# The second single batch in twos of tiles, its tokens turned by VectorE in 32x32 blocks and small transfers

## The chip, the cores and the metric

The kernel runs on one core of a Trainium2 chip. The engines that matter are TensorE (PE in the profile, with its weight loads PEld), VectorE (DVE), ScalarE (ACT), GpSimd (POOL) and SyncE (SP). SP and POOL issue the DMAs here, each from its own queue. The metric is the device time of one execution in microseconds, the median of the timed runs.

## What is computed

`x` has 8 batches of 4096 tokens with 192 channels, all float32. A causal convolution with seven taps per head (8 heads of 24 channels, the taps softmaxed) is followed by a mixing over tokens and a mixing over channels, each with a residual:

```python
w = softmax(weight)                                   # 8 heads x 7 taps
xc[b, s] = sum over k of w[head, k] * x_padded[b, s + k]
h = relu(xc^T @ w_tok1) @ w_tok2                      # 4096 -> 256 -> 4096, over tokens
u = xc + h^T
out = u + relu(u @ w_ch1) @ w_ch2                     # 192 -> 1536 -> 192, over channels
```

## The kernel before

**Batches and tiles.** The eight batches go in five groups, `GROUPS = [[0], [1], [2, 3], [4, 5], [6, 7]]`: two single batches and then three pairs. A batch has NT = 8 tiles of 512 tokens, and a tile TJ = 4 blocks (j) of 128 tokens. Products run in a split form: a float32 operand is a high part plus a low part, and three products (high by high, high by low, low by high) give one.

**Stage 1 of a group** (`stage1`, L627) is the convolution of a whole batch or pair (first tap on ACT, L660, six more on VectorE, L662, in 16 pieces of the batch, stored to DRAM as `xcd`), and the first token mixing: 16 chunks of `w_tok1` are loaded (`t1_load`, L703), multiplied by the convolved tokens (`mix`, L764 for a single batch, L768 to L770 for a pair, 24 products of three kinds in the two halves of a chunk) and accumulated. For group 2 the weights come unsplit: ACT makes the high part of a chunk (L732), VectorE the low part (L736), and the convolved tokens are split by ACT (L748) and VectorE (L752). When all chunks are done, L381 and L382 make `h1`, which the second token mixing of that group reads.

**Stage 1 runs as background** of the group before it. Its steps are items with a cost, a lag and sometimes a gate (`class Item`), and the class `Background` puts them into the program between pieces of the tile work: after each piece the tile code calls `bg.fg(pe, dve)` with the piece's rough cost, and `fill` hands out the items that are due by two running sums (`bg.pe`, `bg.dve`). While `bg.tiled` is set (all of `channel1`) no item with TensorE work is handed out. Between `bg.hold()` and `bg.release()` transfers of the background wait. `bg.finish(group)` puts in whatever is left of a group's stage 1; it is called before the last tile of the group ahead.

**The tile work.** Each turn of the main loop (L1224) does one tile of one batch: `channel1` (L1039; 12 pairs of `w_ch1` blocks, products L1017, high part of the result by ACT L1056, low part by VectorE L1057), then, where the next tile is due, `mix2` of that (L891), then `channel2` (L1080; products L1091 and L1092, adds L1097 and L1098) in two halves of two blocks, and the store of the result (L1100). For a group of two batches the second product has a form with half tiles, `channel2_halves` (L1063, L1074), in those tiles in which no turn is due.

**How a next tile is made ready.** `mix2` adds the second token mixing to the convolved tokens in `u`, 128 tokens by 2x192 columns per block; `channel1` needs the channels on the partitions, so the tokens have to be turned. There are two ways, and a group uses one throughout:

- *Single batch* (groups 0 and 1). `mix2` has two products per block and half of `w_tok2` (L912, L913), two VectorE adds (L927, L928) and an ACT copy (L929): the two copies of the tile lie in `u` side by side. `transposed` (L942) turns each of the three 128-column parts with four TensorE transposes into PSUM (L950), from which ACT takes the high part (L952) and VectorE the low part (L953). It stands between the two halves of `channel2`.
- *Pair* (groups 2 to 4). `u[:, :, :, i]` holds batch i of the pair. `mix2` has three products (L915 to L917), one VectorE add (L932) and, per block, one VectorE transpose of 32x32 blocks into `own_hi` (L933). `blocks_sent` (L956) moves the blocks to their places in `other` with 16 DMAs of 48 KB, eight issued by SP and eight by POOL (L966). `parted` (L971), called in the third quarter of `channel2`, splits them (three ACT casts L979, three VectorE subtractions L981), copies the upper half of the partitions for the swapped layout (two ACT copies of 64x1536, L984) and the lower half by two POOL DMAs (L986). The first tile of the two reads `own` with its first 64 partitions and `swapped` with its last 64, the second tile the other way round.

In the pair's main loop the turn is at the second tile: the next pair's `mix2` and `blocks_sent` follow its `channel1`, and the transfers of the background are held from there until the blocks are sent.

**Loads.** `load_tile` (L868) loads the `w_tok2` part of a tile (`t2`, two DMAs, L875) and its convolved tokens (`u`, L879) on SP, one tile ahead. In group 2's stage 1 (that is, while batch 1 runs) three of the 16 chunk buffers of `w_tok1` lie in the memory of `other` (the "spare"), which batch 1 doesn't need: the last three chunks are loaded early into it (L714 to L722).

## Time and profile before

| | |
|---|---|
| median of 3 runs | 2035.07 us (2034.55 to 2036.43) |
| profiled execution: its span | 2031.3 us |
| PE busy | 2019.2 us |
| DVE busy | 1453.6 us |
| ACT busy | 761.4 us |
| POOL busy | 218.7 us |
| mean traffic | 127 GB/s |

The span of the profiled execution runs from its first to its last instruction; its own device time is not listed, and the median of the timed runs is 3.8 us longer than its span. Batch 0 takes the stretch up to about 335 us of the trace, batch 1 that from there to about 590 us, and the three pairs the rest. The places that matter are the tiles of batch 1: a tile without chunks of stage 1's product is `channel1`, `mix2` and `channel2` with the transposes in it; the next six have two chunks each; and the last four chunks stand together at the batch's end, ahead of its last tile.

### The profile page before, as it was taken

To read this page: it belongs to the slowest core of one execution; us is meant where nothing else is said; L and a number is where in the kernel's file an instruction comes from. 1 tells how busy PE (TensorE), PEld (TensorE's weight loads), DVE (VectorE), ACT (ScalarE), POOL (GpSimd) and SP (SyncE) were. 2 spreads that over 40 slices of the span, in tenths; PEclk is the share of its full clock that TensorE was granted. 3 is DMA by queue.
4 is the path that set the end of the run, shared out by engine and by line. 5 is a ranking of instruction groups with operands and counts; after the bars stand their busy time and mean duration, and the time that the engine had idled before them with its cause. 6 is when DMAs were issued, how large, how long until landed. Compare 5 with 4: busy or idle time off the path is not lost.

```text
span 2031.3 us, 42018 instructions
## 1 busy us (share of the span) xinstructions
PE 2019.2 (99%) x17435; PEld 1860.7 (92%) x17435; DVE 1453.6 (72%) x2877; ACT 761.4 (37%) x1305; POOL 218.7 (11%) x383
## 2 busy tenths in 40 slices
PE   9899999999999999999999999999999999999999
PEld 9889999999999998999999999999999999999998
DVE  8799998999659999757985689545555545555554
ACT  4575544443433434233333334233232332233322
POOL 0100000000011011100111110111111011111110
PEclk9999999999999999999999999999999999999999
DMA  9845346454434567324654434533222233233310
GB/s 308 292 158 170 119 156 201 146 168 157 142 118 134 165 199 202 104 82 128 169 162 115 108 109 134 150 87 84 73 61 56 71 84 84 76 84 84 84 48 17
DMA packets 289230, 258.39 MB, mean 127 GB/s; under 512 B 209360, under 2 KB 238544, under 8 KB 289040
## 3 DMA queue, kind: packets, MB, share of 16 engines
q1 hardware_dynamic: 265120, 168.00, 29.3%
q0 software_dynamic: 23920, 87.71, 14.0%
q8 instruction: 138, 2.26, 0.5%
q14 instruction: 52, 0.43, 0.1%
HBM read 146.60 MB, written 71.30 MB: 107 GB/s over the span
## 4 chain that ended last, share of the span: by engine, by line
PE 94%; DVE 4%; ACT 1%; DMA 0%; issue 0%; SPq 0%; POOL 0%; DVEq 0%; POOLq 0%; ACTq 0%
PE ps_x L1017 37%; PE ps_x L1091 17%; PE ps_x L1074 16%; PE ps_x L1092 8%; PE ps_x L915 2%; PE ps_x L917 2%; PE ps_x L916 2%; PE ps_a L768 2%; PE ps_a L769 2%; PE ps_a L770 2%; DVE xc L662 1%; PE ps_a L452 1%; PE ps_x L912 1%; PE ps_x L950 1%; PE ps_a L764 1%; PE ps_x L521 1%
## 5 line engine op out<-in xcount | busy, mean ns | idle before, releaser
L1056 ACT ACTIVATE hh<-ps_x 128x512 fp32r<-128x512 f32 x756 | 410.7, 596 | 744.3 <-PE ps_x L1017 744.2
L1057 DVE SCALAR_TENSOR_TENSOR hl<-ps_x,hh 128x512 fp32r<-128x512 f32 x756 | 484.9, 686 | 198.5 <-ACT hh L1056 197.0
L1091 PE MATMUL ps_x<-w,hh 128*128 128x384 f32 x1872 | 538.4, 359 | 0.1
L1092 PE MATMUL ps_x<-w,hl 128*128 128x192 f32 x1872 | 468.6, 250 | 0.0
L1017 PE MATMUL ps_x<-other,w_hi 64*128 64x512 f32 x1728 | 450.3, 389 | 0.6 <-DVE osb L1098 0.5
L662 DVE SCALAR_TENSOR_TENSOR xc<-raw,cw,xc 128x384 f32<-128x384 f32 (+1 forms) x768 | 389.4, 562 | 9.4 <-ACT xc L660 9.4
L1092 PEld LDWEIGHTS ps_x<-w,hl 128*128 128x128 f32 x1872 | 357.4, 191 | 0.0
L1091 PEld LDWEIGHTS ps_x<-w,hh 128*128 128x128 f32 x1872 | 351.5, 188 | 0.7 <-DVE hl L1057 0.7
L1017 PEld LDWEIGHTS ps_x<-other,w_hi 64*128 64x128 f32 x1728 | 314.1, 184 | 32.1 <-PE ps_x L1017 0.9
L1017 PE MATMUL ps_x<-own_hi,w_hi 64*128 64x512 f32 x1440 | 333.0, 394 | 1.2 <-DVE hl L1057 0.9
L1074 PE MATMUL ps_x<-w,hh 64*128 64x384 f32 x2304 | 329.6, 355 | 0.0
L1017 PE MATMUL ps_x<-own_hi,w_lo 64*128 64x512 f32 x1440 | 325.8, 387 | 0.0
L1017 PE MATMUL ps_x<-own_lo,w_hi 64*128 64x512 f32 x1440 | 325.6, 387 | 0.0
L1074 PE MATMUL ps_x<-w,hl 64*128 64x192 f32 x2304 | 292.2, 247 | 0.0
L1017 PEld LDWEIGHTS ps_x<-own_hi,w_hi 64*128 64x128 f32 x1440 | 210.0, 185 | 36.1 <-issue 6.3
L1017 PE MATMUL ps_x<-other,w_lo 64*128 64x512 f32 x864 | 242.1, 386 | 0.0
L1017 PEld LDWEIGHTS ps_x<-own_hi,w_lo 64*128 64x128 f32 x1440 | 215.7, 185 | 28.5
L1017 PEld LDWEIGHTS ps_x<-own_lo,w_hi 64*128 64x128 f32 x1440 | 215.8, 185 | 28.2
L1074 PEld LDWEIGHTS ps_x<-w,hl 64*128 64x128 f32 x2304 | 226.0, 188 | 1.0 <-DVE hl L1057 0.2
L1074 PEld LDWEIGHTS ps_x<-w,hh 64*128 64x128 f32 x2304 | 222.1, 184 | 0.9
L1017 PEld LDWEIGHTS ps_x<-other,w_lo 64*128 64x128 f32 x864 | 159.0, 184 | 16.1
L1097 DVE TENSOR_TENSOR osb<-ps_x,u 128x192 f32<-128x192 f32 x156 | 55.4, 355 | 143.6 <-PE ps_x L1092 143.0
(143 smaller groups left out, 2154.8 us busy)
## 6 DMA issues: line engine op xcount, KB each, us to landing
raw<-in_x_dram SPq DMA_DIRECT2D x56, 672.0 KB, 7.5
t<-t2d SPq DMA_DIRECT2D x64, 512.0 KB, 5.3
out_dram<-osb POOLq DMA_DIRECT2D x63, 384.0 KB, 4.5
u<-xcd SPq DMA_DIRECT2D x62, 384.0 KB, 6.5
xcd<-xc POOLq DMA_DIRECT2D x28, 768.0 KB, 7.6
t<-t1p SPq DMA_DIRECT2D x32, 512.0 KB, 5.4
other<-own_hi SPq DMA_DIRECT2D x192, 48.0 KB, 2.1
other<-own_hi POOLq DMA_DIRECT2D x192, 48.0 KB, 2.0
```

The costliest lines, as they stand in the source:

```text
L662: nc.vector.scalar_tensor_tensor(out=dst, in0=src, scalar=cw[:, h, k:k + 1], in1=dst, op0=ALU.mult, op1=ALU.add)
L768: nc.tensor.matmul(out=ps, lhsT=wh, rhs=xh, start=a, stop=False)
L769: nc.tensor.matmul(out=ps, lhsT=wh, rhs=xl, start=False, stop=False)
L770: nc.tensor.matmul(out=ps, lhsT=wl, rhs=xh, start=False, stop=z)
L915: nc.tensor.matmul(out=ps[:, :n], lhsT=wh, rhs=hh, start=a, stop=False)
L1017: nc.tensor.matmul(out=ps, lhsT=w1[w][rows, c, p * P:(p + 1) * P], rhs=t[h][v][rows, c], start=n == 0, stop=n == len(prods) - 1,)
L1056: nc.scalar.activation(out=h["hh", f], in_=ps, func=AF.Relu)
L1057: nc.vector.scalar_tensor_tensor(out=h["hl", f], in0=ps, scalar=0.0, in1=f32(h["hh", f]), op0=ALU.max, op1=ALU.subtract)
L1074: nc.tensor.matmul(out=ps[:, :m], lhsT=h[part, f][ks, ts], rhs=w2[ks, f, :m], start=n == 0 and part == "hh", stop=z and part == "hl",)
L1091: nc.tensor.matmul(out=ps[:, :2 * D], lhsT=h["hh", f][:, ts], rhs=w2[:, f, :], start=n == 0, stop=False)
L1092: nc.tensor.matmul(out=ps[:, :D], lhsT=h["hl", f][:, ts], rhs=w2[:, f, :D], start=False, stop=z)
L1097: nc.vector.tensor_tensor(out=rows(osb[:, j]), in0=rows(ps[:, :D]), in1=tokens(u, i)[:, j], op=ALU.add)
```

## The change

Batch 1 goes in four units of two tiles, each laid out as a pair is: `u[:, :, :, i]` is tile i of the unit. Its tokens are turned as the pairs' are.

- A table `units` replaces the count of tiles: a unit is a list of (batch, tile). `load_unit` replaces `load_tile`; `w_tok2` parts are loaded a tile at a time by `load_t2`. For the first unit both parts are needed at once, and the second goes into the two buffers `xhl` of stage 1.
- `mix2` takes `i`: two adds in place on `u[:, :, :, i]` (L923, L924 after), no copy by ACT, and for the second tile of a unit the VectorE transposes of the whole block (`turn_blocks`, L943 after). For the first tile of a next unit it follows the `channel1` of the first tile of this unit, for the second tile that of the second. For the first unit of batch 1 both stand at batch 0's last tile.
- `blocks_sent` (L976 after) and `parted` (L989 to L996 after) take the place of `transposed` at the turns to units; `bg.hold()` and `bg.release()` stand around these turns too.
- Batch 1's second product is `channel2` in all tiles, as it was.
- `other` is now in use during batch 1, so the three spare buffers are gone: the chunks of `w_tok1` for group 2 are loaded three ahead, into three buffers, to the end.

```diff
-            elif gi == 2:
-                if n < LAST:
-                    t1 = mp.tile([P, MJ, 2, JT], F32R, name="t1", bufs=AHEAD[nb])
-                else:
-                    if "spare" not in done:
-                        done["spare"] = mp.tile([P, 2, ND, TT], F32R, name="other").rearrange("p a c t -> p (a c t)")
-                    w = MJ * 2 * JT
-                    t1 = done["spare"][:, (n - LAST) * w:(n - LAST + 1) * w].rearrange("p (j t m) -> p j t m", t=2, m=JT)
-                nc.sync.dma_start(out=f32(t1[:, :, 1:2]), in_=part(top))
             else:
                 t1 = mp.tile([P, MJ, 2, JT], F32R, name="t1", bufs=AHEAD[nb])
-                nc.sync.dma_start(out=f32(t1), in_=part(t1p))
+                if gi == 2:
+                    nc.sync.dma_start(out=f32(t1[:, :, 1:2]), in_=part(top))
+                else:
+                    nc.sync.dma_start(out=f32(t1), in_=part(t1p))
...
-            if n + AHEAD[nb] < (LAST if gi == 2 else NJ // MJ):
+            if n + AHEAD[nb] < NJ // MJ:
                 mixing.append(Item(lambda: t1_load(n + AHEAD[nb])))
-            if gi == 2 and n % 2 and n // 2 < NJ // MJ - LAST:
-                mixing.append(Item(lambda: t1_load(LAST + n // 2)))
...
+    def load_t2(q, pool, second=False):
+        q2, h = q // 2, q % 2
+        if second:
+            homes = [pool.tile([P, 2, MJ * 2, D], F32R, name="xhl", bufs=2) for _ in range(KC)]
...
+        for kc in range(KC):
+            nc.sync.dma_start(out=f32(parts[kc]), in_=t2d[q2][:, kc, :, h * TJ:(h + 1) * TJ, :])
...
+            if i is not None:
+                one = uj[:, :, i]
+                nc.vector.tensor_tensor(out=one, in0=rows(ps[:, :D]), in1=one, op=ALU.add)
+                nc.vector.tensor_tensor(out=one, in0=rows(ps[:, D:2 * D]), in1=one, op=ALU.add)
+                if turned is not None:
+                    turn_blocks(uj, turned, j)
+                continue
...
+        elif gi:
+            units.append([[(bs[0], q + i) for i in range(2)] for q in range(0, NT, 2)])
...
-                if turn and pairs:
+                if turn and blocks:
                     z = up.tile([P, ND * NQ, P], F32, name="own_hi")
-                    mix2(*nxt, *loaded, turned=z)
+                    t2, v = loaded
+                    if tiles:
+                        for k in range(2 - len(t2), 2):
+                            mix2(nxt[0], following[k][1], t2[k - 2], v, i=k, turned=z if k else None)
+                    else:
+                        mix2(nxt[0], nxt[1], t2[0], v, turned=z)
                     other = blocks_sent(z)
                     bg.release()
...
+                elif blocks and nxt[0] == gi and len(bs) == 1:
+                    mix2(gi, following[0][1], loaded[0][0], loaded[1], i=0)
+                    loaded = [load_t2(following[1][1], sp)], loaded[1]
```

**What moves.** Only the program between batch 0's last tile and the end of batch 1's seventh differs. Three places:

VectorE at the turn from batch 0 to batch 1, behind the second block's adds of `mix2` (`xc` and `raw` are the background's convolution, `osb` the adds of `channel2`). Before:

```order
L927 TENSOR_TENSOR u<-ps_x,u 128x3x64
L928 TENSOR_TENSOR u<-ps_x,u 128x3x64
L662 SCALAR_TENSOR_TENSOR xc_3070<-raw_3400,cw,xc_3070 128x16x24 x4
L1097 TENSOR_TENSOR osb<-ps_x,u 128x192
L1098 TENSOR_TENSOR osb<-ps_x,osb 128x192
L662 SCALAR_TENSOR_TENSOR xc_3070<-raw_3400,cw,xc_3070 128x16x24 x4
L1097 TENSOR_TENSOR osb<-ps_x,u 128x192
L1098 TENSOR_TENSOR osb<-ps_x,osb 128x192
L662 SCALAR_TENSOR_TENSOR xc_3070<-raw_3400,cw,xc_3070 128x16x24 x2
L953 TENSOR_TENSOR own_lo<-ps_x,own_hi 128x512 x3
```

After, from the last block of the second tile's `mix2` on:

```order
L923 TENSOR_TENSOR u<-ps_x,u 128x3x64
L924 TENSOR_TENSOR u<-ps_x,u 128x3x64
L943 STREAM_TRANSPOSE own_hi<-u 128x12x32
L1107 TENSOR_TENSOR osb<-ps_x,u 128x192
L1108 TENSOR_TENSOR osb<-ps_x,osb 128x192
L1107 TENSOR_TENSOR osb<-ps_x,u 128x192
L1108 TENSOR_TENSOR osb<-ps_x,osb 128x192
L991 TENSOR_TENSOR own_lo<-other,own_hi 128x512 x3
```

The background's convolution is out of this stretch, and the subtractions of `parted` (L991) read `other`, which the transfers fill, where L953 read the transposes' PSUM.

VectorE at the end of batch 1's seventh tile (`t_...` are chunks of `w_tok1`, `xhl` the split tokens). Before:

```order
L1097 TENSOR_TENSOR osb<-ps_x,u 128x192
L1098 TENSOR_TENSOR osb<-ps_x,osb 128x192
L752 TENSOR_TENSOR xhl<-xc_5281,xhl 128x768
L1097 TENSOR_TENSOR osb<-ps_x,u 128x192
L1098 TENSOR_TENSOR osb<-ps_x,osb 128x192
L736 TENSOR_TENSOR other<-other 128x2x256
L752 TENSOR_TENSOR xhl<-xc_5281,xhl 128x768
L736 TENSOR_TENSOR other<-other 128x2x256
L752 TENSOR_TENSOR xhl<-xc_5281,xhl 128x768
L382 SCALAR_TENSOR_TENSOR h_486<-ps_a_3724,h_486 128x384
```

After:

```order
L1107 TENSOR_TENSOR osb<-ps_x,u 128x192
L1108 TENSOR_TENSOR osb<-ps_x,osb 128x192
L661 SCALAR_TENSOR_TENSOR xc_5653<-raw_5815,cw,xc_5653 128x16x24 x2
L1107 TENSOR_TENSOR osb<-ps_x,u 128x192
L1108 TENSOR_TENSOR osb<-ps_x,osb 128x192
L744 TENSOR_TENSOR xhl<-xc_5653,xhl 128x768
L728 TENSOR_TENSOR t_6211<-t_6211 128x2x256
L744 TENSOR_TENSOR xhl<-xc_5653,xhl 128x768
L728 TENSOR_TENSOR t_6241<-t_6241 128x2x256
L744 TENSOR_TENSOR xhl<-xc_5653,xhl 128x768
L728 TENSOR_TENSOR t_6348<-t_6348 128x2x256
L744 TENSOR_TENSOR xhl<-xc_5653,xhl 128x768
```

The last pieces of the convolution (L661) have come into the last half of `channel2`; four splits of tokens (L744) and three of weights (L728) now stand behind its last adds, where two of each stood there before.

SP's queue there. Before (the three loads into the spare, `other<-t1d`, stand further ahead):

```order
L723 DMA t_5478<-t1d 128x2x256
L723 DMA t_5502<-t1d 128x2x256
L723 DMA t_5694<-t1d 128x2x256
L875 DMA t_5705<-t2d 128x2x512 x2
L879 DMA u<-xcd_76 128x12x64
L723 DMA t_5890<-t1d 128x2x256
L875 DMA t_6075<-t2d 128x2x512 x2
L879 DMA u<-xcd_76 128x12x64
L875 DMA t_6483<-t2d 128x2x512 x2
L879 DMA u<-xcd_77 128x12x64 x2
L966 DMA other<-own_hi 32x3x128 x8
```

After:

```order
L976 DMA other<-own_hi 32x3x128 x8
L649 DMA raw_5815<-in_x_dram 128x14x96 x2
L716 DMA t_5912<-t1d 128x2x256
L716 DMA t_5952<-t1d 128x2x256
L716 DMA t_6211<-t1d 128x2x256
L716 DMA t_6241<-t1d 128x2x256
L716 DMA t_6348<-t1d 128x2x256
L869 DMA t_6403<-t2d 128x2x512 x2
L879 DMA u<-xcd_77 128x12x64 x2
L976 DMA other<-own_hi 32x3x128 x8
```

Five chunk loads (L716), to the last chunk, stand together behind a turn's sends (L976) and the last load of `raw`, and the next tile's loads behind them; before, the last four had the loads of a tile among them.

## Rows read from the trace of the kernel before

**Rows 1.** The page: busy time of each engine with its share of the span and its instructions; TensorE's granted clock in 40 slices of the span, in tenths; the chain of work that ended last, by engine.

```profile
PE 2019.2 (99%) x17435; PEld 1860.7 (92%) x17435; DVE 1453.6 (72%) x2877; ACT 761.4 (37%) x1305; POOL 218.7 (11%) x383
...
PEclk9999999999999999999999999999999999999999
...
PE 94%; DVE 4%; ACT 1%; DMA 0%; issue 0%; SPq 0%; POOL 0%; DVEq 0%; POOLq 0%; ACTq 0%
```

**Rows 2.** The waits of PE over the whole span, the longest line: what waited for what, then us in total, times, and the longest.

```profile
PE ps_x L950 <- ACT u L923: 2.3, 2, 2.0
```

**Rows 3.** The timeline of PE from batch 0's last `channel1` to batch 1's first: start, us, engine, line, operation, tiles, count. Where a count is over 1, the row covers that many.

```profile
304.92 0.97 PE L1017 MATMUL ps_x<-own_hi,w_hi 64*128 64x512 f32 x6
...
317.39 0.44 PE L912 MATMUL ps_x<-h,t 128*128 128x384 f32 x1
...
319.75 0.36 PE L1091 MATMUL ps_x<-w,hh 128*128 128x384 f32 x1
...
326.58 1.47 PE L950 MATMUL ps_x<-ident,u 128*128 128x128 f32 x12
327.80 0.42 PE L1091 MATMUL ps_x<-w,hh 128*128 128x384 f32 x1
...
334.92 0.97 PE L1017 MATMUL ps_x<-own_hi,w_hi 64*128 64x512 f32 x6
```

**Rows 4.** The groups by line, of 305 to 578 us: the TensorE transposes of eight tiles. Busy us, mean ns of one, idle before.

```profile
L950 PE MATMUL ps_x<-ident,u 128*128 128x128 f32 x96 | 11.8, 272 | 0.0
```

**Rows 5.** Windows between instructions of PE: window, its length, then busy us (and instructions) of PE, PEld, DVE, ACT and POOL, the granted clock, the share of the DMA engines, GB/s. In this order: batch 0's last `channel1`; its last `channel2` with the twelve transposes; a `channel2` of a pair's turn, which has none; the `channel1` that follows it; a `channel2` of a later pair with two chunks of stage 1's product in it; two whole tiles of batch 1, each with two such chunks; the last four chunks together, up to batch 1's last `channel1`.

```profile
304.92:317.39 12.47, 12.47 (x110) 10.04 (x109) 7.65 (x14) 6.23 (x12) 1.89 (x3) 1.00 0.93 255
...
319.75:334.92 15.17, 15.17 (x111) 15.00 (x109) 14.96 (x34) 4.00 (x9) 0.00 (x0) 1.00 0.22 70
594.60:608.32 13.72, 13.72 (x97) 13.56 (x97) 5.87 (x13) 4.39 (x5) 4.95 (x9) 1.00 0.64 165
608.32:620.72 12.40, 12.40 (x111) 10.23 (x111) 9.99 (x19) 7.47 (x15) 3.33 (x6) 1.00 1.15 286
711.53:729.45 17.92, 17.92 (x123) 17.76 (x122) 15.30 (x30) 6.90 (x10) 6.61 (x12) 1.00 0.80 208
364.92:398.99 34.07, 34.07 (x257) 32.12 (x256) 32.43 (x65) 14.04 (x27) 1.61 (x3) 1.00 0.50 157
467.16:503.39 36.23, 36.23 (x269) 33.53 (x269) 35.85 (x72) 14.53 (x28) 1.63 (x3) 1.00 0.33 112
569.38:577.84 8.46, 8.46 (x50) 8.21 (x48) 4.25 (x7) 2.68 (x4) 1.61 (x3) 1.00 0.82 259
```

**Rows 6.** The timeline of the first turn to a unit of two, that of a pair (batches 2 and 3, second tiles), all engines: the last block's add and transpose, the sends, the splits and copies, and the `channel1` that reads them. In brackets the idle time before and what ended it.

```profile
595.45 0.52 DVE L932 TENSOR_TENSOR u<-ps_x,u 128x384 f32<-128x384 f32 x1
596.00 0.58 DVE L933 STREAM_TRANSPOSE own_hi<-u 128x384 f32<-128x384 f32 x1
...
596.72 5.23 SPq L966 DMA_DIRECT2D other<-own_hi  x8
...
603.90 1.66 ACT L979 CAST own_hi<-other 128x512 fp32r<-128x512 f32 x3 [12.40 <-DMA other<-own_hi]
...
605.59 1.48 ACT L984 CAST other<-own_hi 64x1536 fp32r<-64x1536 f32 x1
...
608.32 0.49 PE L1017 MATMUL ps_x<-other,w_hi 64*128 64x512 f32 x1
```

**Rows 7.** The page's DMA issues: tiles, queue, count, KB each, median us from issue to landing.

```profile
other<-own_hi SPq DMA_DIRECT2D x192, 48.0 KB, 2.1
```

**Rows 8.** The timeline of DVE at the turn from batch 0 to batch 1: first and last of the eight adds of `mix2`, and what follows them.

```profile
319.33 0.35 DVE L927 TENSOR_TENSOR u<-ps_x,u 128x192 f32<-128x192 f32 x1
...
321.69 0.36 DVE L928 TENSOR_TENSOR u<-ps_x,u 128x192 f32<-128x192 f32 x1
321.96 2.20 DVE L662 SCALAR_TENSOR_TENSOR xc<-raw,cw,xc 128x384 f32<-128x384 f32 x4
```

**Rows 9.** The timelines of PE and DVE in a tile of batch 1 with chunks in it: the first product of a `mix2`, and the first and the last of its adds.

```profile
411.46 0.44 PE L912 MATMUL ps_x<-h,t 128*128 128x384 f32 x1
...
414.67 0.35 DVE L927 TENSOR_TENSOR u<-ps_x,u 128x192 f32<-128x192 f32 x1
...
419.15 0.36 DVE L928 TENSOR_TENSOR u<-ps_x,u 128x192 f32<-128x192 f32 x1
```

**Rows 10.** The end of batch 1's seventh tile: DVE's last adds of `channel2` and a split of a weight chunk, then ACT's high part of a weight chunk and DVE's split of tokens; and, from the view of line 723 (the loads of weight chunks), the time from issue to landing.

```profile
569.58 0.36 DVE L1097 TENSOR_TENSOR osb<-ps_x,u 128x192 f32<-128x192 f32 x1 [1.80 <-PE ps_x L1092]
...
570.24 0.68 DVE L736 TENSOR_TENSOR other<-other 128x512 fp32r<-128x512 f32 x1
572.45 0.61 ACT L732 CAST other<-other 128x512 fp32r<-128x512 f32 x1
...
572.58 0.96 DVE L752 TENSOR_TENSOR xhl<-xc,xhl 128x768 fp32r<-128x768 f32 x1 [1.65 <-ACT xhl L748]
...
DMA to landing us min/median/max: 3.1/3.6/5.8
```

**Rows 11.** Windows in batch 0's first tile, columns as in group 5: the second and the seventh us behind the longest wait of PE, which ended at 61.23 us, and a stretch with another wait.

```profile
61.00:62.00 1.00, 0.77 (x4) 0.69 (x5) 0.05 (x1) 0.44 (x2) 1.00 (x2) 0.50 0.98 353
66.00:67.00 1.00, 1.00 (x8) 0.80 (x6) 1.00 (x2) 0.00 (x0) 0.00 (x0) 0.50 1.04 410
...
80.00:82.00 2.00, 0.82 (x6) 0.53 (x4) 1.95 (x3) 0.60 (x1) 0.16 (x1) 1.00 0.39 84
```

More of the change, by code (lines that the diff above doesn't have):

```diff
@@ L162, in conv_mixer_kernel @@
     AHEAD = {1: 5, 2: 3}
-    LAST = NJ // MJ - 3
     PACE = 1.2
@@ L889, in conv_mixer_kernel, with mix2 @@
     NQ = P // QB
-    def mix2(gi, q, t2, u, at_once=False, turned=None, between=()):
+    def mix2(gi, q, t2, u, at_once=False, turned=None, between=(), i=None):
         nb = len(GROUPS[gi])
@@ L1209, in conv_mixer_kernel @@
     starts = {}
+    units = []
+    for gi, bs in enumerate(GROUPS):
+        if len(bs) > 1:
+            units.append([[(b, q) for b in bs] for q in range(NT)])
+        elif gi:
+            units.append([[(bs[0], q + i) for i in range(2)] for q in range(0, NT, 2)])
+        else:
+            units.append([[(bs[0], q)] for q in range(NT)])
     for gi, bs in enumerate(GROUPS):
@@ L1223, in conv_mixer_kernel @@
             loaded = first["next"]
-        for q in range(NT):
-            nxt = (gi, q + 1) if q + 1 < NT else (gi + 1, 0)
-            for i, b in enumerate(bs):
-                turn = i == nb - 1 and nxt[0] < len(GROUPS)
+        for n, unit in enumerate(units[gi]):
+            nxt = (gi, n + 1) if n + 1 < len(units[gi]) else (gi + 1, 0)
+            for i, (b, q) in enumerate(unit):
+                turn = i == len(unit) - 1 and nxt[0] < len(GROUPS)
+                final = last and n + 1 == len(units[gi]) and i + 1 == len(unit)
                 run_ahead(gi)
@@ L1256, in conv_mixer_kernel @@
                         bg.require(("t2", nxt[1] // 2, nxt[1] % 2))
-                    mix2(*nxt, *loaded)
+                    mix2(*nxt, None, loaded[1])
                     mixed[0] = nxt[1]
-                product2 = channel2 if turn or last and q + 1 == NT and i + 1 == nb else channel2_halves
+                elif blocks and nxt[0] == gi and len(bs) == 1:
+                    mix2(gi, following[0][1], loaded[0][0], loaded[1], i=0)
+                    loaded = [load_t2(following[1][1], sp)], loaded[1]
+                product2 = channel2 if turn or final or len(bs) == 1 else channel2_halves
                 if ahead:
                     product2(i, h, u, osb, half[0])
-                if turn and not pairs:
+                if turn and not blocks:
                     abc = transposed(loaded[1])
@@ L1266, in conv_mixer_kernel @@
                     w2_split()
-                if last and q + 1 == NT and i + 1 == nb:
+                if final:
                     for j in range(TJ):
@@ L1273, in conv_mixer_kernel @@
                     if ahead:
-                        if turn and pairs:
+                        if turn and blocks:
                             made = []
```

52 lines of the change are left out of this document (30 added, 22 removed).

## The prediction

> **What bounds the kernel now.** I read the page first, then PE's waits, then windows between PE's own instructions. PE is busy 2019.2 of 2031.3 us, 94% of the chain that ended last is PE, and the granted clock stands at its upper level, 2.4 GHz, in all 40 slices [rows 1]. The longest wait of PE is 2.0 us, at a transpose of the first tile [rows 2]; in every window of batch 1 that I cut, PE's busy time equals the window's length [rows 5]. So in batch 1 what PE does is the time: PE work that goes counts in full, and a new wait of PE counts in full too. VectorE is at 72% over the span, but that is an average: in batch 1's tiles it is busy 32.43 us of 34.07 and 35.85 of 36.23 [rows 5], with PE still not waiting.
>
> The program differs only between batch 0's last tile and the end of batch 1's seventh; the rest cancels.
>
> **The PE work that goes.** Eight tiles were turned by twelve transposes each: batch 0's last, and batch 1's first seven; 96 instructions, 11.8 us of busy time [rows 4]. What they cost PE is better read from whole stretches. `channel2` with transposes took 15.17 us (319.75 to 334.92), without them 13.72 [rows 3, 5]: 1.45 each, for the two tiles without chunks of stage 1, 2.90 together. `channel1` on the pair's layout took 12.40 where on the old one it took 12.47 [rows 5]: 0.07 for each of batch 1's eight tiles, 0.14 for the first and the last of them, which have no chunks (the six others have it in the next term). For the six tiles with two chunks I put the new tile together: 12.40 + 2.36 (`mix2`, 317.39 to 319.75 [rows 3], its products are unchanged) + 17.92 (a `channel2` with two chunks and no transposes) = 32.68, against 34.07 measured [rows 5]: 1.39 each, 8.34. Sum 2.90 + 0.14 + 8.34 = 11.4 us. From below, by 1.22 us a tile between the two products around the transposes (326.58 to 327.80 [rows 3]), it is 9.8; from above, by the busy time and the 0.56 of `channel1`, 12.4.
>
> ACT loses four copies a tile, VectorE keeps eight adds a tile. Over two tiles VectorE loses three subtractions and gains four transposes of 0.58 us [rows 6], about even. I cost these at nothing as long as VectorE keeps up (a rival, below). The `w_tok2` and token loads are the same in bytes, one tile later at most; SP waits longer in its queue, priced with the chunks.
>
> **What a turn costs now.** With transposes the next `channel1` needed only PE, ACT and VectorE. Now it needs a chain outside PE, whose length is read at the first pair's turn [rows 6]: the last VectorE transpose ended at 596.58; SP issued its eight sends from 596.72 on, for 5.23 us; the first cast began at 603.90, when they had landed; the copy of the high parts ran from 605.59 to 607.07. That is 10.5 us from the last transpose to `channel1`'s first operand. Each block lands 2.1 us after its issue [rows 7], so the queue's eight issues are the larger part. The copy ended 1.25 us ahead of `channel1` at 608.32.
>
> *Turn from batch 0 to batch 1.* Both tiles' `mix2` stand behind batch 0's last `channel1`. In before the eight adds started 1.94 us after `mix2` began at 317.39 (at 319.33) and let the next instruction in at 321.96 [rows 3, 8]. After, the second tile's four blocks follow, each with two adds and a transpose; by 0.66 us for two adds (2.63 us for eight) and up to 0.61 for a transpose with its latency that is 1.27 a block, so the last transpose ends near 321.96 + 5.1 = 327.05, and the operand is ready at 337.55. PE has 2 x 2.36 + 13.72 us from 317.39 on, to 335.83. PE waits **1.7 us**. If the chain is as short as 10.25 us it is 1.5, and if it needs 12.5 us (the sends of POOL or the low copies deciding), 3.7.
>
> *Turns inside batch 1* (second, fourth and sixth tile). Only one `mix2` precedes: the last transpose ends 1.94 + 5.1 = 7.0 us after it begins, the operand is there at 17.5, and PE has 2.36 + 17.92 = 20.28 us of work. A margin of 2.8 us: no wait. This needs VectorE to come to the adds at once; in the order after, no background row stands between the last low part of `channel1` and these adds.
>
> **What the end of stage 1 costs now.** Held transfers and the missing spare push group 2's convolution and chunks later. In before the last four chunks ran without a gap, 8.46 us, 569.38 to 577.84 [rows 5]. After, the first of the four splits of tokens stands behind VectorE's last adds of `channel2`, which wait for PE. In before the first of these adds began 0.20 us after the chunks did, and two adds later, at 570.24, the engine was free [rows 10]; with a split of 0.96 us the first chunk's operand is there 1.8 us after PE comes for it: **1.8 us** of wait. Then the last weight chunk: with three buffers its load can be issued only when PE has done the first of the four, 2.1 us later. Landing takes 3.1 / 3.6 / 5.8 us (least, median, most), its high part 0.61 on ACT, its low part 0.68 and a split 0.96 on VectorE [rows 10]: 5.9 us by the median, against 4.2 us of PE work on the two chunks between: **1.6 us**, 1.1 by the least and 3.8 by the most. Together 3.4 (2.9 to 5.6). Nobody else waits for it: the `mix2` that reads the result stands behind a whole `channel1`.
>
> **Sum.** 11.4 - 1.7 - 3.4 = 6.3 us. The profiled execution's span 2031.3 becomes 2025.0; the runs' median is 3.8 above the span (the profiled execution's own time is not listed), so 2025.0 + 3.8 = **2028.8 us**.
>
> A measured row says that twelve transposes and their place cost the bound engine 1.45 us, while VectorE's transposes of a block take 0.58 and cost PE nothing [rows 5, 6]. The Trainium skill's page "VectorE: DVE Perf Modes", in "Rules for kernel authors", tells the other way: for a full 128x128 transpose use TensorE if PSUM will do as its destination, since VectorE's path gives blocks of 32x32 only. By that rule TensorE's transposes should stay and the change brings nothing or a loss, 2035.1 us or more; by the rows it removes 11.4 us from PE. No row before shows a single batch turned by VectorE; the mechanism by which the rule would come true is rival 4.
>
> **Rivals.**
>
> 1. *The clock falls at a new wait.* In the first tile PE waited 2.0 us, and behind that the granted clock was 0.50, its lower level of 1.2 GHz, at 61 to 62 us and still at 66 to 67; at the other stretch, with PE busy 0.82 of 2 us, it stayed at 1.00 [rows 2, 11]. A new wait of 1.7 or 1.8 us lies between these two. Some 6.5 us at half speed lose 3.3 us: 2032.1 for one fall, 2035.4 for two. Against it: here PE is dense on both sides, there it was not. Chance 0.21.
> 2. *The waits don't show*, because VectorE and the transfers are sooner than I chain them. Then the whole 11.4 stands: 2023.7, or up to 2027 with one of the waits. Chance 0.13.
> 3. *VectorE becomes the bound in tiles two to six*, so that the change does not do what it says: PE's gain turns into waiting. VectorE's work of 32.4 us a tile now meets 32.68 us of PE. Some 0.7 to 1.6 us lost in each of five tiles give 2032 to 2037. For it: the convolution starts later and has to fit into fewer tiles. Against it: at 35.85 of 36.23 PE didn't wait [rows 5]. Chance 0.12.
> 4. *Slower: the turns inside batch 1 come late.* In a tile of before `mix2` began at 411.46 and its last add ended at 419.51, 8.0 us after it, where at the turn of batch 0 it took 4.7 [rows 8, 9]: background work of VectorE stood between. Such a delay of 3.4 us is over the margin of 2.8. If it comes at the three turns, with the larger of PE's delays and a clock that falls each time, 3 x (2 + 3.3) = 16 us are lost: 2044.7. It decides from a loss of 3.4 us at each turn on, where the time passes 2039.1. Against it: the order has no such row there. Chance 0.08.
>
> The forecast itself has 0.46. With each of its terms at the better end it is 2027.1 (12.4 - 1.5 - 2.9 = 8.0 saved), with each at the worse 2034.6 (9.8 - 3.7 - 5.6 = 0.5).
>
> **How the numbers follow.** About 0.2% (4.07 us) is what a measurement of this kernel can tell from no change, so faster means below 2031.0 and slower above 2039.1. Faster: 0.42 of the forecast, rival 2 and 0.02 of the others, 0.57. Same: rival 1, most of rival 3 and the forecast's upper end, 0.34. Slower: rival 4 and the worst of rival 3, 0.09. The range 2025.0 to 2036.0 holds the forecast, rival 1, most of rival 3 and the upper half of rival 2, about 0.83.
>
> **What would show it.** In the profile after: no TensorE transposes between 305 and 578 us; tiles with two chunks 32.7 us long with PE busy throughout; a wait of PE for ACT's copy at batch 1's first `channel1`, 1.5 to 3.7 us; no such wait at its other turns; two waits among the last four chunks, the first for VectorE's split of tokens, the second for the last weight chunk; clock 1.00 throughout. The forecast is wrong if tiles stay at 34 us, if PE waits at the turns inside batch 1, or if a window behind a wait shows 0.50.

## The result, and the profile after

The changed kernel takes 2050.51 us in the median of 4 runs (2049.67 to 2052.15), the kernel before beside it 2034.81 (2034.23 to 2036.43): a ratio of 1.008, 95% interval 1.0065 to 1.0094. It is 15.7 us slower where 6.3 less were forecast. The profiled execution has a span of 2048.7 us, 17.4 more than before. In the runs further down one execution of run 9 (2149.19 us) and one of run 10 (4967.53 us) lie far above the others of the same kernel and are left out of the medians.

The page after: busy time by engine, and the chain that ended last.

```profile
PE 2017.8 (98%) x17339; PEld 1854.5 (91%) x17339; DVE 1453.2 (71%) x2881; ACT 754.4 (37%) x1269; POOL 241.9 (12%) x423
...
PE 88%; DVE 5%; DMA 4%; ACT 1%; SPq 1%; issue 1%; POOL 0%; ACTq 0%; DVEq 0%; POOLq 0%
```

Against [rows 1], DMA has come into the chain with 4%. PE's busy time has hardly fallen (2019.2 to 2017.8), and its idle time has grown from 12.1 to 30.9 us. The next view, windows after (columns as in [rows 5]), shows where: batch 1's second to sixth tile, its seventh up to the last four chunks, and these chunks.

```profile
366.80:399.56 32.76, 32.76 (x246) 30.17 (x246) 27.45 (x56) 16.19 (x26) 8.30 (x14) 1.00 0.35 98
399.56:439.04 39.48, 35.98 (x246) 31.59 (x246) 33.88 (x68) 10.14 (x20) 2.18 (x4) 0.96 0.82 243
439.04:471.77 32.73, 32.73 (x245) 30.15 (x244) 29.12 (x59) 15.73 (x26) 8.34 (x14) 1.00 0.37 113
471.77:510.67 38.90, 35.95 (x245) 32.59 (x245) 31.70 (x63) 10.61 (x20) 2.19 (x4) 0.91 0.84 234
510.67:543.40 32.73, 32.73 (x245) 30.16 (x244) 25.64 (x50) 12.77 (x23) 7.71 (x13) 1.00 0.37 107
543.40:578.34 34.94, 32.75 (x229) 28.91 (x228) 32.06 (x62) 14.15 (x24) 3.32 (x7) 1.00 0.52 143
578.34:597.52 19.18, 11.28 (x48) 9.88 (x48) 6.82 (x10) 4.58 (x8) 3.45 (x6) 0.77 1.00 293
```

The second, fourth and sixth tile, whose ends are the turns, take 32.73 to 32.76 us with PE busy throughout: to 0.1 us the 32.68 put together ahead. The third and the fifth, each the first behind a turn, take 39.48 and 38.90: 6.7 and 6.2 us too many, with the DMA engines busy 0.82 and 0.84 of the time where the tiles beside them have 0.35 to 0.37. The last four chunks take 19.2 us where they took 8.46 [rows 5]. These three places are 23.6 us over what their work needs. The seventh tile, which is the first behind the third turn inside batch 1, took 34.94 us up to these chunks; the ledger below comes to it.

What PE waited for there, and the clock behind the waits (the waits of PE over the whole span; then windows of 5 us):

```profile
PE ps_a L760 <- ACT xhl L740: 6.5, 2, 6.3
PE ps_x L1027 <- DVE hl L1067: 4.6, 4, 3.0
PE ps_x L912 <- DVE hl L1067: 2.8, 1, 2.8
...
PE ps_x L1027 <- ACT other L994: 1.6, 2, 1.3
```

```profile
415.00:420.00 5.00, 5.00 (x26) 3.98 (x27) 3.64 (x7) 4.13 (x8) 0.53 (x1) 0.68 0.82 199
485.00:490.00 5.00, 2.75 (x8) 2.06 (x8) 3.58 (x7) 5.00 (x11) 0.53 (x1) 0.65 1.09 239
490.00:495.00 5.00, 4.97 (x24) 4.97 (x25) 4.86 (x13) 1.07 (x3) 0.00 (x0) 0.67 1.00 289
590.00:595.00 5.00, 1.98 (x5) 1.58 (x6) 1.65 (x2) 1.35 (x2) 0.53 (x1) 0.50 1.16 322
```

Three waits (3.0, 2.8 and 6.3 us), and a clock below its upper level behind each (the windows of 5 us mix the two levels). The view names VectorE's low part for two of them; VectorE is not where they begin. The timeline of the third tile, PE, DVE, ACT and SP, leads back step by step:

```profile
414.27 0.50 PE L1027 MATMUL ps_x<-own_hi,w_hi 64*128 64x512 f32 x1 [3.03 <-DVE hl L1067]
...
413.52 2.48 DVE L1067 SCALAR_TENSOR_TENSOR hl<-ps_x,hh 128x512 fp32r<-128x512 f32 x4 [3.62 <-ACT hh L1066]
...
412.37 0.62 ACT L724 CAST t<-t 128x512 fp32r<-128x512 f32 x1 [7.32 <-DMA t<-t1d]
412.90 3.03 ACT L1066 ACTIVATE hh<-ps_x 128x512 fp32r<-128x512 f32 x6
...
386.57 5.09 SPq L976 DMA_DIRECT2D other<-own_hi  x8
392.09 3.14 SPq L649 DMA_DIRECT2D raw<-in_x_dram  x2
395.40 10.28 SPq L716 DMA_DIRECT2D t<-t1d  x2
405.72 1.07 SPq L869 DMA_DIRECT2D t<-t2d  x2
406.90 6.87 SPq L879 DMA_DIRECT2D u<-xcd  x2
```

Read from below: SP sends the blocks, then the raw loads that the turn had held, then two weight chunks, whose issue alone took 10.28 us behind the raw loads (9.33 of it is one of the two); then `w_tok2` and tokens. ACT reached the cast of a chunk (L724) early and waited 7.32 us for it. Behind that cast in ACT's queue stood `channel1`'s evictions (L1066), six of which then ran at once; VectorE waited 3.62 us for them, and PE 3.03 us for room in PSUM. In before ACT never waited for a chunk load. In the fifth and the seventh tile the same cast waited again:

```profile
484.27 0.62 ACT L724 CAST t<-t 128x512 fp32r<-128x512 f32 x1 [4.94 <-DMA t<-t1d]
...
555.93 0.62 ACT L724 CAST t<-t 128x512 fp32r<-128x512 f32 x1 [3.92 <-DMA t<-t1d]
```

From issue to landing the chunk loads took (view of their line, after):

```profile
DMA to landing us min/median/max: 3.0/8.6/18.2
```

That was 3.1 / 3.6 / 5.8 in [rows 10]. At the batch's end the last chunk alone did the same (timelines of PE, ACT and SP):

```profile
592.71 0.69 PE L760 MATMUL ps_a<-xhl,t 128*128 128x384 f32 x1 [6.33 <-ACT xhl L740]
...
591.31 0.62 ACT L724 CAST t<-t 128x512 fp32r<-128x512 f32 x1 [8.21 <-DMA t<-t1d]
...
582.25 0.36 SPq L716 DMA_DIRECT2D t<-t1d  x1
582.66 2.67 SPq L869 DMA_DIRECT2D t<-t2d  x2
585.38 6.50 SPq L879 DMA_DIRECT2D u<-xcd  x2
```

Issued at 582.25 us, when the first of the four chunks was done, it shared the DMA engines with the next group's `w_tok2` and token loads (293 GB/s in that window) and came some 9 us later.

### The profile page after: what moved, and what is told of

Read it like the earlier page. It is cut to its first block, busy times and chain, and to the rows that moved or that the text cites. A ratio compares the mean times of both kernels' runs of the same rounds, so it can differ in the third digit from the quotient of the medians.

```text
span 2048.7 us, 41977 instructions
## 1 busy us (share of the span) xinstructions
PE 2017.8 (98%) x17339; PEld 1854.5 (91%) x17339; DVE 1453.2 (71%) x2881; ACT 754.4 (37%) x1269; POOL 241.9 (12%) x423
## 4 chain that ended last, share of the span: by engine, by line
PE 88%; DVE 5%; DMA 4%; ACT 1%; SPq 1%; issue 1%; POOL 0%; ACTq 0%; DVEq 0%; POOLq 0%
PE ps_x L1027 34%; PE ps_x L1084 16%; PE ps_x L1101 16%; PE ps_x L1102 7%; DMA t<-t1d 3%; PE ps_x L915 2%; PE ps_x L917 2%; PE ps_x L916 2%; PE ps_a L761 1%; PE ps_a L760 1%; PE ps_a L762 1%; DVE hl L1067 1%; DVE xc L661 1%; PE ps_a L451 1%; PE ps_a L756 1%; PE ps_x L912 1%
## 5 line engine op out<-in xcount | busy, mean ns | idle before, releaser
L1066 ACT ACTIVATE hh<-ps_x 128x512 fp32r<-128x512 f32 x756 | 410.0, 596 | 745.6 <-PE ps_x L1027 745.6
L1027 PE MATMUL ps_x<-other,w_hi 64*128 64x512 f32 x2016 | 527.5, 390 | 2.1 <-ACT other L994 1.6
L1027 PEld LDWEIGHTS ps_x<-other,w_hi 64*128 64x128 f32 x2016 | 367.3, 185 | 42.1 <-ACT other L994 2.6
L661 DVE SCALAR_TENSOR_TENSOR xc<-raw,cw,xc 128x384 f32<-128x384 f32 (+1 forms) x768 | 388.1, 563 | 9.4 <-ACT xc L659 9.4
L1027 PE MATMUL ps_x<-other,w_lo 64*128 64x512 f32 x1008 | 283.2, 387 | 0.0
L1027 PEld LDWEIGHTS ps_x<-other,w_lo 64*128 64x128 f32 x1008 | 186.1, 185 | 19.9
L976 POOL DMA_DIRECT2D other<-own_hi x224 | 121.7, 552 | 478.3 <-DVE own_hi L943 351.5
```

The lines of the kernel that those rows point to most:

```text
L661: nc.vector.scalar_tensor_tensor(out=dst, in0=src, scalar=cw[:, h, k:k + 1], in1=dst, op0=ALU.mult, op1=ALU.add)
L976: queue.dma_start(out=f32(other[q * QB:(q + 1) * QB, 1, :, i * P:(i + 1) * P]), in_=blocks[i * QB:(i + 1) * QB, q])
L1027: nc.tensor.matmul(out=ps, lhsT=w1[w][rows, c, p * P:(p + 1) * P], rhs=t[h][v][rows, c], start=n == 0, stop=n == len(prods) - 1,)
L1066: nc.scalar.activation(out=h["hh", f], in_=ps, func=AF.Relu)
```

## The experiments

**Theory A:** what comes late is what is loaded behind a turn. The hold gathers the raw loads and lets them go together with the chunk, `w_tok2` and token loads; ACT's queue is in order, so a background step on it that waits for one of these holds `channel1`'s evictions. The last chunk is a case of its own: without the spare it can't be loaded early. **Rival B:** three buffers without the spare are too few throughout. **Rival C:** VectorE, filled by the later convolution, holds PE.

**1. The kernel before, without the spare.**

```diff
-            if n + AHEAD[nb] < (LAST if gi == 2 else NJ // MJ):
+            if n + AHEAD[nb] < NJ // MJ:
                 mixing.append(Item(lambda: t1_load(n + AHEAD[nb])))
-            if gi == 2 and n % 2 and n // 2 < NJ // MJ - LAST:
-                mixing.append(Item(lambda: t1_load(LAST + n // 2)))
```

> The kernel before with one part of the change alone: no spare, all 16 weight chunks of group 2 three ahead in three buffers. Theory A (the changed kernel loses because chunk loads come late only where they are queued right behind the raw loads that the turn had held, and ACT's cast of the late chunk stands ahead of channel1's evictions): here nothing is held in batch 1, the chunk loads stand some 14 us behind the raw loads, so no tile of batch 1 grows; only the last chunks may wait, 2 to 6 us with the clock: 2036 to 2041. Rival B (three buffers without the spare are too few by themselves): the tiles with chunks stall here too, +10 us or more, 2045 and above.

2039.4 us against 2033.37, ratio 1.0028 (1.0016 to 1.0039). No tile with chunks grew; the chunk loads landed in 3.0 / 3.5 / 5.8 us. The last tile with the last chunks took 45.93 us instead of 40.34, with these waits (530 to 590 us) and a clock of 0.66 in the 5 us at 580:

```profile
579.62 0.44 PE L761 MATMUL ps_a<-xhl,t 128*128 128x384 f32 x1 [2.98 <-ACT xhl L741]
580.61 0.69 PE L762 MATMUL ps_a<-xhl,t 128*128 128x384 f32 x1 [0.55 <-DVE xhl L745]
```

So the spare by itself is worth 5.6 to 6 us, all at the end: B falls for the tiles.

**2. Casts later in the changed kernel.**

```diff
-                mixing.append(Item(lambda: t1_hi(*a), lag=300, gate=lambda: done["t1", n] + (5e3 if n else 14e3)))
+                mixing.append(Item(lambda: t1_hi(*a), lag=300, gate=lambda: done["t1", n] + 16e3))
```

> The changed kernel with one number different: the planner counts 16 us instead of 5 from a chunk load's issue to its cast on ACT (the first chunk 16 instead of 14). Theory A: ACT no longer waits ahead of channel1's evictions, the third and the fifth tile of batch 1 go from 39.5 and 38.9 us to 32.7, with the clock at 1.00: 13 us less, 2036 to 2039; the 19.0 us of the last four chunks stay. Rival C (VectorE, filled by the later convolution, is what holds PE in these tiles): the waits for the low parts stay, 2048 to 2052.

2043.91 us, 6.6 less than the changed kernel, half of what A gave. Most of that came at the end: from the seventh tile to batch 1's last `channel1` it took 50.8 us instead of 54.1. The fifth tile still took 39.25 us and the third 37.79, but for another load (waits of PE, 300 to 610 us):

```profile
PE ps_x L912 <- DMA t<-t2d: 4.4, 4, 1.9
```

This is `w_tok2` itself, which stands behind the chunk loads in SP's queue. Neither theory had that as expected; it is A's mechanism with the next load in the row.

**3. No hold at batch 1's turns.**

```diff
-                if turn and blocks:
+                if turn and blocks and not tiles:
                     bg.hold()
```

> The changed kernel without hold and release at batch 1's turns (pairs keep them). If the hold makes the bunch of raw and chunk loads, the chunk casts wait no more, the convolution is done earlier and the last chunks take under 12 us: 2030 to 2040, less what the turns lose where block sends stand behind raw loads (1 to 5 us each). If the hold has nothing to do with it: 2048 to 2052, with the same waits of ACT for the chunk loads.

2046.33 us, a miss by both. In the third tile ACT waited for no chunk, in the fifth 0.75 us instead of 4.94, and the third fell to 34.47 us. But at the turn from batch 0 ACT waited 2.8 us for a raw load that now stood ahead (PE 1.9 us, a slow clock behind it, that tile 35.0 us instead of 30.9), and the turn into the fifth tile waited 2.6 us for sends behind raw loads; this tile, which also took in a part of a third chunk, needed 39.0. The last chunk came late as before (ACT 5.28 us, PE 3.39). In addition the pairs, where the program is the same, took some 7 us more than in the changed kernel, 5.4 of them at the late turn that run 8 shows.

**4. Chunk loads issued by POOL.**

```diff
-                    nc.sync.dma_start(out=f32(t1[:, :, 1:2]), in_=part(top))
+                    nc.gpsimd.dma_start(out=f32(t1[:, :, 1:2]), in_=part(top))
```

> The changed kernel with group 2's chunk loads issued by POOL instead of SP; nothing else. If it is the place behind the raw loads in SP's queue that makes them late (issues of up to 9.3 us there), they land in 3 to 6 us and the waits of the third and fifth tile go: 2036 to 2040. If the transfers are late because the DMA engines are full or the buffers come free late, nothing changes: 2048 to 2052.

2053.42 us (two executions): nothing gained. A chunk's issue now took 0.7 us, but from issue to landing the loads took (view of their line in this run):

```profile
DMA to landing us min/median/max: 3.4/8.0/10.8
```

The median is close to the 8.6 of the changed kernel. ACT still waited 8.4 us for chunks (26.6 in the changed kernel) and now 10.2 us for raw loads, where it had waited for none; the third tile fell to 35.4 us, the fifth rose to 41.9. The place in SP's queue alone does not make the loads late. The Trainium skill's page "DMA: Bandwidth & Descriptors" says in "Issuing engines are not separate DMA queues" that DMAs from any issuer run on the same 16 engines and interleave; this run agrees, with 8.0 us to landing from POOL's queue.

**5. Casts later, and the next `w_tok2` part ahead of the raw loads.**

```diff
                     other = blocks_sent(z)
+                    early = None
+                    if tiles and nxt[1] + 1 < len(units[nxt[0]]):
+                        early = load_t2(units[nxt[0]][nxt[1] + 1][0][1], sp)
                     bg.release()
...
```

> The changed kernel with the later cast (16 us counted from a chunk load's issue) and, besides, the next unit's first part of w_tok2 loaded right behind the block sends, ahead of the raw loads that are released there. Theory A (what comes late is what stands in SP's queue behind the released raw loads: chunk loads first, then w_tok2): with both moved PE no longer waits in the third and the fifth tile of batch 1, each 32.7 to 34 us instead of 37.8 and 39.3; 8 to 11 us less than with the later cast alone, 2033 to 2036; the last four chunks as slow as before, 17 to 19 us. Rival C (VectorE holds PE there): the tiles stay above 37 us, 2042 to 2045.

2050.40 us in only two runs (2045.7 and 2055.1): a miss. `w_tok2` was in time, but ACT now waited 7.5 us for raw loads at the convolution's first tap, and the tiles took 39.7 and 41.1 us. They stay above 37 us, as C has it, but behind ACT's waits for raw loads. Putting one load ahead makes the next one late.

**6. The last two chunks early, in the `w_tok2` tile.**

```diff
+                if gi == 2 and n >= NJ // MJ - 2:
+                    if "spare" not in done:
+                        done["spare"] = mp.tile([P, KC, 2, TJ, P], F32R, name="t2").rearrange("p a r j m -> p (a r j m)")
...
-            if n + AHEAD[nb] < NJ // MJ:
+            if n + AHEAD[nb] < NJ // MJ - (2 if gi == 2 else 0):
...
+                    if tiles and nxt[1] + 1 == len(units[1]):
+                        for k in (14, 15):
+                            starts[2][2](k)
```

> The changed kernel with the last two weight chunks of group 2 loaded early, into the memory of the w_tok2 tile, which batch 1 no longer needs after its last turn; nothing else. Theory A: the last four chunks take 10 to 12 us instead of 19.0, at most one wait of 2 us for VectorE's split is left, and the clock doesn't fall there: 8 us less, 2040 to 2044; third and fifth tile as slow as before. If the convolution, done late, is what makes the end long: 16 us or more there, 2048 to 2051.

2042.75 us, 7.8 less than the changed kernel; the last chunks took 9.9 us (578.29 to 588.14) with one wait of 1.1 us and the clock at 1.00. So the long end was the last load, not the late convolution.

**7. The edits of runs 5 (the later cast is part of it) and 6 together.**

> The changed kernel with all three: later cast, early load of w_tok2, last two chunks in the w_tok2 tile. Theory A: the 11.4 us of PE work show, less the first turn's 1.3 us and some 2 us at the last chunks: 2024 to 2029, faster than the kernel before by 0.2 to 0.5%. Rival C: not below 2036.

2040.38 us, a miss of what A gave. The time is within C's bound, but the waits are again ACT's: the end is short, the third and fifth tile took 36.9 and 40.5 us, and ACT waited 10.7 us for raw loads. Three repairs of single loads don't remove the bunch.

**8. The bunch taken apart:** as run 6, casts 10 us from a load's issue, and the hold only at the turn from batch 0.

```diff
-                if turn and blocks:
+                if turn and blocks and (gi == 0 or not tiles):
                     bg.hold()
```

> The changed kernel with the last two chunks in the w_tok2 tile, casts counted 10 us from a later load's issue (the first 14 as before), and the hold kept at the turn from batch 0 but not at the turns inside batch 1. Theory A (released raw loads bunch with chunk and w_tok2 loads behind a turn): the third and fifth tile fall from 36.2 and 40.1 us (with the two chunks moved alone) to 34 or less; in exchange block sends stand behind raw loads in SP's queue and the next tile's first product waits 1 to 2.5 us at one or two turns, with a fall of the clock at one: 2034 to 2040. If the bunch is not the cause: the third and fifth tile stay over 36 us, 2041 to 2045.

**9. The same, with the hold put back** (run after the others, the casts and the two chunks unchanged).

> The version with the hold at the first turn only, with the hold put back at all turns of batch 1; casts 10 us from a load's issue and the last two chunks in the w_tok2 tile stay. If the hold makes the third and the fifth tile long: 36 us or more each again, 2039 to 2043. If the later casts were what mended them: 2033 to 2036, tiles under 35.5 us.

```diff
-                if turn and blocks and (gi == 0 or not tiles):
+                if turn and blocks:
                     bg.hold()
```

With the hold 2045.5 us (median of four; ratio 1.0050, 1.0035 to 1.0065), longer than expected; third and fifth tile, and ACT's waits for chunks from 300 to 610 us:

```profile
402.61:441.83 39.22, 36.05 (x245) 31.68 (x244) 33.93 (x67) 10.13 (x20) 2.19 (x4) 0.96 0.82 245
474.59:513.93 39.34, 36.17 (x245) 32.87 (x244) 31.87 (x64) 10.71 (x20) 2.20 (x4) 0.91 0.83 233
...
ACT t L730 <- DMA t<-t1d: 17.8, 3, 7.1
```

Without it 2034.47 us and these windows (third, fourth, fifth tile; seventh with the last chunks), then the same wait of ACT, and PE's in the third tile:

```profile
398.95:434.45 35.50, 34.27 (x246) 30.48 (x245) 34.93 (x70) 11.57 (x22) 2.18 (x4) 1.00 0.73 212
434.45:467.18 32.73, 32.73 (x245) 30.17 (x244) 28.91 (x58) 15.39 (x25) 8.31 (x14) 1.00 0.54 160
467.18:499.96 32.78, 32.78 (x245) 30.19 (x245) 31.93 (x64) 11.05 (x21) 2.19 (x4) 1.00 0.82 231
...
532.70:573.31 40.61, 39.22 (x277) 36.18 (x276) 35.82 (x66) 16.13 (x28) 6.16 (x10) 1.00 0.45 150
...
ACT t L730 <- DMA t<-t1d: 2.3, 1, 2.3
...
404.36 0.47 PE L1033 MATMUL ps_x<-other,w_hi 64*128 64x512 f32 x1 [0.81 <-DVE osb L1114]
```

The hold decides: the two kernels differ by nothing else, and with it ACT waits 7.05, 4.90 and 5.86 us for a chunk in the third, fifth and seventh tile, as in the changed kernel (7.32, 4.94, 3.92), without it in none of them. The cast 10 us from the issue mends nothing while the hold stays.

C falls for the fifth tile: VectorE is busy 31.93 us there without the hold, more than the 31.70 of the changed kernel, and PE doesn't wait. It does not fall for the third. That took 35.50 us where 34 or less were expected, with VectorE busy 34.93 of them and PE waiting for an add (L1114) that stood behind background convolution. By this profile VectorE is what holds PE there once the loads are mended, with the tile 2.8 us over 32.7; no run took that work away to show it.

From batch 0's last `channel1` to batch 1's last the run without it takes 268.4 us (304.92 to 573.31) where before took 272.9. Yet the whole was no faster than before (ratio 1.0001, 0.9992 to 1.0010): behind that the profile is 6.9 us longer than before's. Of these 4.8 were lost at a late pair turn. POOL stopped in the middle of its eight sends, waiting for nothing that the profile shows, PE waited at the tile behind it, and the clock fell (timelines of POOL and PE, then a window):

```profile
1910.87 1.62 POOL L982 DMA_DIRECT2D other<-own_hi  x3 [2.62 <-issue]
...
1917.15 0.50 PE L1033 MATMUL ps_x<-own_hi,w_hi 64*128 64x512 f32 x1 [0.55 <-ACT own_hi L995]
1919.69 0.49 PE L1033 MATMUL ps_x<-other,w_hi 64*128 64x512 f32 x1 [2.04 <-ACT other L1000]
...
1920.00:1925.00 5.00, 5.00 (x32) 3.96 (x30) 1.63 (x3) 2.10 (x3) 0.58 (x1) 0.66 1.04 225
```

**10. As run 8, with SP's sends issued by ACT** at batch 1's turns.

```diff
-                    other = blocks_sent(z)
+                    other = blocks_sent(z, nc.scalar if tiles else nc.sync)
```

> The same, and the eight sends of a turn in batch 1 that SP issued are issued by ACT, so that they stand behind no raw load. Theory A: the waits at the turns go as well, tiles of 32.7 to 34 us: 2027 to 2034. If it is the full DMA engines and not SP's queue that delay the sends: as the run without this, 2034 to 2040.

2035.74 us (median of nine), ratio 1.0007 (0.9997 to 1.0017): the turns were not what was left, and the second expectation holds. From batch 0's last `channel1` to batch 1's last it took 271.3 us instead of 268.4, and the same wait of 2.04 us stood in the pairs.

**11, 12. As run 8, with small memsets on POOL,** to move its instructions.

```diff
+                if gi == 1 and n == 3 and i == 1:
+                    pad = sp.tile([P, 8], F32, name="pad")
+                    for _ in range(6):
+                        nc.gpsimd.memset(pad, 0.0)
```

> The version with the hold at the first turn only, and 6 small memsets of a scratch tile added to POOL's queue in batch 1's last tile; no other instruction differs. In that version batch 1 took 268.4 us instead of 272.9, yet the whole time was the same as before, because POOL paused for 2.6 us in the middle of its eight sends of one late pair turn (waiting for nothing that the profile shows), PE waited 0.55 and 2.04 us at the tile behind it and the clock fell there. If the pause comes with the place in POOL's instruction stream, it moves by six instructions, off that turn, and the time is 2028 to 2031. If it belongs to that turn's transfers, it stays: 2033 to 2036.

> The same with 12 memsets: the pause moves by twelve instructions; where it falls on no turn's sends 2028 to 2031, where it falls on another turn's 2033 to 2036. If it belongs to the transfers: 2033 to 2036, pause at the same turn.

2033.71 and 2032.22 us, ratios 0.9999 (0.9990 to 1.0008) and 0.9998 (0.9989 to 1.0007). The second lies between the two ranges expected. The pause stayed at the same turn in both, 2.61 us before its last three sends: it does not come with the place in the instruction stream. The clock fell behind it in the profile with 12 and not in the one with 6.

**13. As run 8, with two output stores moved from POOL to SP.**

```diff
-                    store_out(gi, b, q, osb, range(TJ), nc.gpsimd)
+                    store_out(gi, b, q, osb, range(TJ), nc.sync if gi == 1 and q >= 6 else nc.gpsimd)
```

> The version with the hold at the first turn only, and the output stores of batch 1's last two tiles issued by SP instead of POOL. If POOL's pause of 2.6 us in the late pair turn comes after a given amount of DMA work that POOL has issued, it moves to a later DMA, off that turn's sends, the wait of 2.0 us behind it goes, and the time is 2028 to 2032, below the kernel before. If not, 2032 to 2035.

2029.09 us against 2033.17, ratio 0.9980 (0.9971 to 0.9989): faster than the kernel before. That it lies at the predicted 2028.8 is luck: this kernel has four edits more than the forecast one, and gains and losses of its own. At that turn POOL's eight sends ran through:

```profile
1904.01 4.36 POOL L982 DMA_DIRECT2D other<-own_hi  x8 [16.69 <-DVE own_hi L949]
...
1915.47 0.54 POOL L1002 DMA_DIRECT2D other<-own_hi  x1 [7.10 <-ACT other L1000]
```

A pause now falls into the sends of another turn; PE waits 2.04 us behind that one, and the clock stays up:

```profile
1023.83 3.79 POOL L982 DMA_DIRECT2D other<-own_hi  x7 [1.53 <-issue]
```

Two more pauses, which cost PE nothing, stood in runs 8, 11 and 12 behind the second and the fourth send of their turns (1.56 us at 712 and 1.54 at 1341 us in run 8). In run 13 they stand behind the fifth and the seventh (713 and 1341 us). So two pauses moved by three sends each, and that of the late turn out of its sends. In this one test the pauses move with the DMA work that POOL has issued. What they are stays open.

## Why the prediction was wrong

- **What bounds the kernel, and the 11.4 us of PE work that go:** right. The tiles at whose end a turn stands take 32.73 us with PE busy throughout, and the forecast for them was 32.68.
- **The turn from batch 0, 1.7 us of wait:** right; 1.30, for ACT's copy, as chained.
- **No wait at the turns inside batch 1:** right, 0.31 us in all. Rival 4 had the loss at these turns, in the adds' delay. The time came close to what that rival gave (2044.7), but not by its mechanism.
- **The step that failed** is the one on what moves outside PE: that ACT and VectorE cost nothing as long as VectorE keeps up, and that SP waiting "longer in its queue" is "priced with the chunks". I priced a late chunk only at the batch's end. Between the tiles the same load is cast by ACT ahead of `channel1`'s evictions, and there it cost 6.7 and 6.2 us in the third and fifth tile and 3.1 in the seventh's `channel1`, where the sum had nothing. The order showed the raw and chunk loads in a row behind the sends; I read it for the last chunk alone. Runs 8 and 9, which differ by the hold alone, show the cause to be the hold.
- **The last chunks, 3.4 us:** the mechanism (a split behind VectorE's adds, then the last load) was right, the size not. The splits' wait was 1.3 us (0.18 and 1.09) instead of 1.8; the last load took some 9 us where I took 3.6 from a quiet stretch and 5.8 as the most, and the clock fell. The term of 1.6 us for the last load was a wait of 6.3. The window grew by 10.7 us, of which 7.9 are PE's idle time. Run 1 puts the same step, without the rest of the change, at 5.6 with the clock.
- **The clock (rival 1):** the mechanism was right and came three times, at waits longer than those I had priced. It stood behind each of the long waits and was no case of its own.
- **VectorE as the bound (rival 3):** not what made the tiles long. PE's waits name it, but in the long ones it waited for ACT. It was not nothing either: `channel2` of the seventh tile took 19.44 us instead of 17.92 with VectorE busy 18.52, and in run 8 the third tile stayed 2.8 us over 32.7 with VectorE busy 34.93 of 35.50.
- **The Trainium skill's rule for 128x128 transposes** ("VectorE: DVE Perf Modes", "Rules for kernel authors"), by which TensorE should keep them: the changed kernel's time is where that rule had it, a loss, but not by what the rule or rival 4 names. The blocks' way home was hidden but for 1.3 us, and run 13, which turns by VectorE and has four more edits, is 4.1 us faster than the kernel with TensorE's transposes. The loss came from the loads around the way home.

The ledger by the profiles: from batch 0's last `channel1` to batch 1's last, 272.92 us became 291.98, 19.1 more. The third and fifth tile give 13.0 and the last chunks 10.7. Another 4.6 us were lost in the seventh tile ahead of them: it has no `mix2`, so 12.40 + 17.92 = 30.3 us of work took 34.9. Of these 3.1 are in its `channel1`, where ACT waited 3.92 us for a chunk, and 1.5 in its `channel2`, where PE waited for VectorE (0.77 us the longest). That is 28.3, and the first turn's 1.3 makes 29.6. Against it stand the 11.4 us of PE work; they leave 18.2 of the 19.1. The spans differ by 1.7 us less than the 19.1. Behind the stretch the program is the same, and there the changed kernel took 1451.2 us, before 1453.5; 2.4 us of difference stand in two tiles of before's first pair (794 to 861 us). One execution of each shows no more.

## What to carry to other kernels

An edit that takes work from the bounding engine still has to be priced on the queues that feed it: for every load that it makes late, look up which engine waits for it in order, and what stands behind that wait. A landing time read in a quiet stretch doesn't hold where a release sends several loads at once. Transfers held back around a short critical chain come back together: here the hold paid at the turn from batch 0, where the chain had no slack (35.0 us without it in run 3, 30.9 with it in run 8, two kernels that differ in other edits too), and cost 10 to 11 us at the turns where it had 2.8 (run 9 against run 8). An engine that stands behind the one that waits can still be the next bound: with the loads mended, the profile has VectorE as that in one tile.

## What the runs showed of the hardware

- A wait of PE of 1.9 to 3.0 us between dense stretches (1.86 in run 3, 2.8 and 3.0 in the changed kernel) was enough for the clock to fall to its lower level, but not each time: behind the wait of 2.04 us at the late turn it fell in the profiles of runs 8, 10 and 12 and not in that of run 11, nor behind an equal wait in run 13. Executions of one kernel differ by some 4 us: run 12 gave 2031.25 to 2032.22 six times and 2033.36 to 2035.76 five times. The fall alone does not explain that, for the profile of run 12, in which the clock fell, is of a 2031.31.
- The issue of a DMA can itself block: one chunk load took 9.33 us to issue on SP right behind 1.3 MB of raw loads, where single ones took 0.36 in a quiet place. Issued by POOL (run 4) none took more than 0.74, and they landed no sooner in the median (8.0 us against 8.6).
- POOL pauses of 1.3 to 2.6 us stand in the middle of its sends with no wait in the profile (before has one of 5.08 and one of 4.21 us behind other DMAs of POOL); they moved when two stores were taken from its queue (two of them by three sends), and not with 6 or 12 memsets put into it.
